# A second expert chosen with the first, and empty rows written as whole rows: layout and request order in a fused attention and mixture-of-experts kernel

## The chip, the cores and the metric

The kernel runs on one core of one Trainium2 chip. The metric is the device time of one execution in microseconds, as the median of several runs; lower is better. Three runs of the kernel before gave 1181.35, 1182.36 and 1184.68 us, so the median is 1182.36 us.

## The reference

The computation has three parts in a row, all in float32.

```python
# attention: x [8,8,512,64], state [8,8,32,64]; scale = 1/8
xread = softmax(scale * x @ state.T) @ state          # 512 rows per batch and head
sread = softmax(scale * state @ x.T) @ x              # 32 rows per batch and head
x = concat([xread, sread], axis=2) -> [8*544, 512]    # heads side by side: 4352 tokens
# first layer: 512 -> 1536 -> 512
x = ((x @ w_a) * (x @ w_b)) @ w_out
# second layer: 8 experts, 512 -> 1024 -> 512, one expert per token
logits = x @ w_gate;  e = argmax(logits, axis=1)
gate = softmax(logits)[e];  eom = sigmoid(x @ w_output_gate)[e]
out[token] = gate * eom * (relu(x @ w1[e]) @ w2[e])
```

The rows that go to each expert depend on the data. With the inputs of the reference the counts of the eight experts are 1082, 32, 576, 64, 512, 1024, 512, 550 over all 4352 tokens, and 1024, 0, 512, 0, 512, 1024, 512, 512 over the 4096 tokens of `xread` alone.

## The kernel before

Phase 1 goes over the 8 batches. For each it computes the attention and the first layer for 512 `xread` tokens; the 8 x 32 `sread` tokens are kept and done together at the end (`main_sr`, 256 tokens). As each group of tokens is done, `Phase1.gate` finds its logits, the expert of each token, a count per expert (`cum`) and so each token's row in `ysort`, a buffer in DRAM that holds the tokens sorted by expert with room for 4608 rows (CAP) per expert. A row is written in four pieces of 130 floats (520 bytes: 128 values of the token, its scale, its number). The layout of `ysort` before is four planes, one per piece: piece `a` of row `r` stands at plane `a`, row `r`. The pieces are scattered from GpSimd by indirect DMAs (L799), 128 pieces each; 136 of them in all, the last eight for the `sread` tokens.

Phase 2 multiplies the sorted rows by the experts' weights, 256 rows at a step, and scatters the results to `out`. Each float32 product is made from a high and a low part, so w1, w2 and the tokens are split by ScalarE (high) and VectorE (low) before use. A half step takes 64 rows. The last step of an expert reads past its last token, so the rows behind each expert's end, 128 of them, are first written with zeros and an invalid token number. That is `pads` (L1059): nine DMAs from the sync engine, one per expert and a second one for the first expert, each 4 x 128 pieces of 520 bytes out of the tile `zrow` (one row of 130 floats per partition, broadcast to the four planes).

Before the phase 2 loop there is a prelude, lines 1777 to 1829, written out by hand, in which two steps (-2 and -1) of the largest expert are run while the counts, the order of the experts and the table of steps are worked out by VectorE in `table`, a generator that the prelude advances stage by stage (`stage()`). The expert of these two steps is chosen earlier, in `early` / `choose` (L858), while `main_sr` still runs, from the counts of the 4096 `xread` tokens: `eoh` marks it, `esel` carries its number and its rows to the sync engine. The sync engine then asks for its w1 and w2 and for its rows (`fetch_pre(0)`, `fetch_pre(1)`).

The sync engine's requests stand in one queue, in this order before the change: w1 of the first expert, `fetch_pre(0)`, w2 of the first expert, `fetch_pre(1)`, then, once the order of all experts is known (third stage of `table`), w2 of the second expert into `raw2` (`load_rank`, L1094), the nine pads, and `fetch_pre(2)`, which reads the rows of step 0. Reads of `ysort` are ordered after all earlier writes to it; the scatters and the pads are declared free of order among themselves (`disjoint`).

The prelude ends with: two of the four splits of the second expert's w2, `turn(0)` (VectorE turns the rows that `fetch_pre(2)` brought), `pre1(3)` (first product, its relu by ScalarE and its low part by VectorE), `parts` (split of the turned rows), the last w2 split, and `pre2(-1, 2)`. `pin` (L657) keeps TensorE, ScalarE, VectorE and the sync engine in the order of the source there. `m.run()` (L1274) then opens one block (L1322) in which each engine runs its own loop with semaphores written by hand. The block is entered by all engines together, when their earlier work is done.

In the loop GpSimd fetches rows (`Phase2.fetch`, L926): four DMAs of 512-byte pieces, one per plane, and one for scale and token number (`gt`). It also issues the scatters to `out`, as it does for the prelude's first step in `preout` (L1054), where the second scatter is ordered behind the first.

Of the kernel before, what the change touches and what calls it, by code (L numbers as in the profile page):

```python
# [18 lines left out]
P = 128  # L19
# [8 lines left out]
NE = 8  # L28
# [4 lines left out]
CAP = NT + 256  # L33
RB = DM // 4 + 2
YW = 16 * RB
PADID = 1 << 20
# [15 lines left out]
class Phase1:  # L52
# [7 lines left out]
    def consts(self):  # L60
# [18 lines left out]
        for g in range(4):  # L79
            sl = slice(32 * g, 32 * g + 32)  # L80
            nc.gpsimd.iota(self.ids[sl, 0 : 16 * NB], [[ST, NB], [1, 4], [P, 4]], base=0, channel_multiplier=4)
            nc.gpsimd.iota(self.ids[sl, 16 * NB :], [[ST, NB]], base=S, channel_multiplier=1)
            nc.gpsimd.memset(self.aoff[sl], float(g * NE * CAP))
# [141 lines left out]

    def disjoint(self, i):
        i = getattr(i, "ins", i)
        self.tc.declare_no_dep(i, group="scatter", reason="disjoint rows")
        self.tc.add_to_no_dep_group("scatter", i)

# [441 lines left out]
    def gate(self, b, T):  # L672
# [116 lines left out]
        def spread():  # L789
            n = 4 * T  # L790
            ps = self.aux("ps_sp")
            nc.tensor.matmul(
                out=ps[:, 0 : 2 * n], lhsT=self.turnto, rhs=st["z"].rearrange("p t g -> p (t g)"), start=True, stop=True
            )
            du = sm("gdu", [n], U32)
            nc.vector.tensor_scalar(out=du, in0=ps[:, 0:n], scalar1=self.aoff[:, 0:1], scalar2=None, op0=ALU.add)
            nc.vector.tensor_copy(out=blocks[:, :, RB - 2 : RB - 1], in_=ps[:, n : 2 * n].unsqueeze(2))  # L797
            for t in range(n):
                self.scatter(  # L799
                    out=self.ysort.rearrange("a r w -> (a r) w"),  # L800
                    out_offset=bass.IndirectOffsetOnAxis(ap=du[:, t : t + 1], axis=0),
                    in_=blocks[:, t, :],
                    in_offset=None,
                    bounds_check=4 * NE * CAP - 1,
                    oob_is_err=False,
                )
# [16 lines left out]
class Phase2:  # L823
# [17 lines left out]
    def early(self):  # L841
# [14 lines left out]
        def choose():  # L856
            self.yin = [ph.yf[:, YW - CH :], ph.yTf[:, 0:CH], ph.yf[:, 0:CH]]
            self.gt = [t(f"gt{i}", [2, 2]) for i in range(4)]  # L858
            step = self.step
# [5 lines left out]
            )  # L865
            mx = t("emx", [1])
            V.tensor_reduce(out=mx, in_=key, axis=AX.X, op=ALU.max)
            self.eoh = t("eoh", [NE])
            V.tensor_tensor(out=self.eoh, in0=key, in1=mx.to_broadcast([P, NE]), op=ALU.is_equal)
            V.tensor_tensor(out=key, in0=self.eoh, in1=self.e8, op=ALU.mult)  # L870
            V.tensor_reduce(out=mx, in_=key, axis=AX.X, op=ALU.add)
            self.esel = t("esel", [2 + NPRE], I32)
            V.tensor_copy(out=self.esel[:, 0:1], in_=mx)
            V.scalar_tensor_tensor(
                out=self.esel[:, 1:], in0=mx.to_broadcast([P, NPRE + 1]), scalar=float(CAP), in1=step, op0=ALU.mult, op1=ALU.add
            )
# [29 lines left out]
    def tiles(self, ctx):  # L906
# [8 lines left out]
        self.tab = p.tile([1, NSTEP, len(FIELDS)], I32, name="tab")  # L915
        self.zrow = p.tile([P, RB], F32, name="zrow")
        self.nc.gpsimd.memset(self.zrow[:, 0 : RB - 1], 0.0)
        self.nc.gpsimd.memset(self.zrow[:, RB - 1 : RB].bitcast(I32), PADID)
# [7 lines left out]
    def fetch(self, e, yin, gt, row, n=2):  # L926

        ys = self.ph.ysort
        rows = P * n if n else HB
        v = ys[:, ds(row, rows), 0 : RB - 2].rearrange("a (t i) x -> a i t x", i=32)  # L930
        x = yin[:, 0 : 4 * rows].rearrange("p (t x) -> p t x", x=P)
        r = [e.dma_start(out=x[32 * a : 32 * a + 32], in_=v[a]) for a in range(4)]  # L932
        v = ys[0, ds(row, rows), RB - 2 : RB]
        if n:
# [124 lines left out]
    def pads(self):  # L1059

        nc = self.nc
        why = "table() bounds every field"
        _, rows = nc.values_load_multi_w_load_instructions(
            self.pad[0:1, 0 : NE + 1],
            engines=[nc.sync.engine],
            min_val=0,
            max_val=NE * CAP - P,
            skip_runtime_bounds_check_because=why,
        )
        for row in rows:  # L1070
            i = nc.sync.dma_start(
                out=self.ph.ysort[:, ds(row, P), :].rearrange("a p w -> p a w"),
                in_=self.zrow.unsqueeze(1).to_broadcast([P, 4, RB]),
            )
            self.ph.disjoint(i)

# [16 lines left out]

    def load_rank(self):  # L1094

        r = self.nc.sync.value_load(self.rtab[0:1, 1:2], min_val=0, max_val=NE - 1)
        self.wload(1, r, self.raw2)

    def table(self, cp):
# [35 lines left out]
        self.pad = cp.tile([P, NE + 1], I32, name="pad")  # L1135
        self.rtab = cp.tile([P, NE], I32, name="rtab")
        pad = t([NE + 1])
# [50 lines left out]
        for v in (nr, gr):  # L1188
            V.tensor_scalar(out=v[:, 0:1], in0=v[:, 0:1], scalar1=1.0, scalar2=None, op0=ALU.max)
        m = t([NE, NE])  # L1190
# [578 lines left out]
def moe_kernel(tc, x, state, w_a, w_b, w_out, w_gate, w_og, w1, w2, out):  # L1769
    w_a, w_b, w_out = (w.bitcast(I32) for w in (w_a, w_b, w_out))  # L1770
    with ExitStack() as ctx:
        pool = lambda n, **k: ctx.enter_context(tc.tile_pool(name=n, bufs=1, **k))
        cp, dp, pg = pool("cp"), pool("dp", space=bass.MemoryType.DRAM), pool("pg")
        ysort = dp.tile([4, NE * CAP, RB], F32, name="ysort")
        ph = Phase1(tc, x, state, w_a, w_b, w_out, w_gate, w_og, ysort, cp, pg)
# [15 lines left out]
        stage()  # L1791
        m.fetch_pre(1)
        m.pre1(0, {15: logits})
        m.pre1(1, {6: gather})
# [70 lines left out]
```

## Time and profile before

The profiled execution took 1187.72 us, of which the span from the first to the last instruction is 1186.0 us; the mean granted TensorE clock is 0.974 of full speed.

| engine | busy us | share of span | instructions |
|---|---|---|---|
| PE (TensorE matmul) | 1123.9 | 95% | 7032 |
| DVE (VectorE) | 648.5 | 55% | 1118 |
| ACT (ScalarE) | 430.1 | 36% | 706 |
| POOL (GpSimd) | 283.9 | 24% | 392 |

The page's 40 slices are 29.65 us each. PE is busy nine tenths or more in nearly all of them; the one slice in the second half that shows less (6 tenths) is the one from 771 to 800 us. The prelude stands from 738 to 796 us and the loop from 798 us to the end. Times in the views below are microseconds from the start of the span; "SPq" is the sync engine's queue, and a bracket at the end of a row gives the engine's idle time ahead of it and what ended it.

### The profile page before, as it was taken

The numbers are of one execution on the slowest core, as the hardware profiler recorded it, in microseconds if no ns is written. First come the engines' busy times: TensorE is split into PE (matmuls) and PEld (weight loads), VectorE is DVE, ScalarE is ACT, GpSimd is POOL, SyncE is SP. The second block draws the span as 40 slices with busy tenths as digits, with TensorE's granted clock in tenths as the row PEclk, the third lists the DMA queues.
The fourth block names the chain that finished last, engine by engine and source line by source line (L and its number), as shares of the span: only waits on it lengthen the run. The fifth ranks groups of instructions, "written<-read, shape, count | busy, mean of one in ns | idle before, by whom it ended". The sixth has DMA issues, their size and how long they took to land. (4 is left out here: it accounts for less than half of the span.)

```text
span 1186.0 us, 19358 instructions
## 1 busy us (share of the span) xinstructions
PE 1123.9 (95%) x7032; PEld 902.4 (76%) x7032; DVE 648.5 (55%) x1118; ACT 430.1 (36%) x706; POOL 283.9 (24%) x392
## 2 busy tenths in 40 slices
PE   3898999999999999999999999969999999999994
PEld 1665777777677777776777799859899998889983
DVE  5889646565464465654754366742442444455463
ACT  4765424333333343333432245321421324142341
POOL 2000005006023050060230524311331232232121
PEclk8898999999999999999999999989999999999997
DMA  6563320302203103020000116369271253536420
GB/s 196 192 226 107 72 38 30 79 3 72 38 15 78 19 30 79 1 72 1 12 26 1 35 33 182 96 128 239 67 204 41 62 166 74 147 89 164 103 97 21
DMA packets 102497, 98.92 MB, mean 83 GB/s; under 512 B 60144, under 2 KB 76048, under 8 KB 102352
## 3 DMA queue, kind: packets, MB, share of 16 engines
q1 hardware_dynamic: 90920, 71.56, 23.2%
q0 software_dynamic: 11168, 25.52, 7.6%
q8 instruction: 72, 1.18, 0.4%
q14 instruction: 73, 0.60, 0.2%
q10 hardware_dynamic: 264, 0.07, 0.0%
HBM read 76.75 MB, written 21.15 MB: 83 GB/s over the span
## 5 line engine op out<-in xcount | busy, mean ns | idle before, releaser
L1009 PE MATMUL ps_h<-yT,w 128*128 128x256 f32 x1536 | 197.5, 285 | 11.0 <-issue 10.0
L1009 PEld LDWEIGHTS ps_h<-yT,w 128*128 128x128 f32 x1536 | 193.9, 193 | 16.8 <-issue 10.8
L1030 PE MATMUL ps_o<-w,hT 128*128 (+1 forms) x768 | 188.1, 394 | 2.3 <-DVE hT L970 2.2
L224 POOL DMA_INDIRECT ysort<-y,gdu x136 | 152.2, 1119 | 149.4 <-DVE y L797 105.8
L528 PE MATMUL ps_y<-gh,wo_h 128*128 128x512 f32 (+1 forms) x432 | 167.1, 392 | 2.1 <-ACT wo_h L218 1.9
L528 PE MATMUL ps_y<-gh,wo_l 128*128 128x512 f32 (+1 forms) x432 | 165.5, 383 | 0.1
L1030 PEld LDWEIGHTS ps_o<-w,hT 128*128 128x128 f32 x768 | 141.5, 190 | 29.8 <-issue 2.4
L528 PE MATMUL ps_y<-gl,wo_h 128*128 128x512 f32 (+1 forms) x432 | 163.3, 379 | 0.0
L516 PE MATMUL ps_ab<-Ah,Mh 128*128 128x512 f32 x384 | 129.6, 418 | 6.8 <-ACT Mh L258 6.8
L501 DVE TENSOR_TENSOR a<-a,ps_ab 128x512 f32<-128x512 f32 x96 | 65.6, 684 | 127.8 <-PE ps_ab L516 126.9
L516 PE MATMUL ps_ab<-Al,Mh 128*128 128x512 f32 x384 | 121.8, 398 | 0.0
L516 PE MATMUL ps_ab<-Ah,Ml 128*128 128x512 f32 x384 | 119.5, 392 | 0.0
L516 PEld LDWEIGHTS ps_ab<-Ah,Mh 128*128 128x128 f32 x384 | 66.7, 191 | 63.1 <-issue 40.2
L990 POOL DMA_INDIRECT out<-yT,gt x37 | 44.6, 1205 | 281.6 <-DVE yT L980 226.7
L964 ACT ACTIVATE hT<-ps_h 128x512 fp32r<-128x512 f32 x64 | 38.0, 593 | 201.5 <-PE ps_h L1009 194.1
L258 ACT ACTIVATE gh<-a 128x512 fp32r<-128x512 f32 (+1 forms) x108 | 65.4, 606 | 106.5 <-DVE a L501 106.5
L528 PEld LDWEIGHTS ps_y<-gh,wo_h 128*128 128x128 f32 x432 | 81.6, 189 | 26.5 <-issue 6.3
L259 DVE TENSOR_TENSOR gl<-a,gh 128x512 fp32r<-128x512 f32 (+1 forms) x108 | 71.1, 658 | 44.6 <-ACT gh L258 44.5
L970 DVE SCALAR_TENSOR_TENSOR hT<-ps_h,hT 128x512 fp32r<-128x512 f32 x64 | 44.0, 687 | 93.7 <-ACT hT L964 93.7
L500 ACT ACTIVATE a<-ps_ab 128x512 f32<-128x512 f32 x96 | 57.5, 599 | 101.4 <-PE ps_ab L516 101.2
L528 PEld LDWEIGHTS ps_y<-gl,wo_h 128*128 128x128 f32 x432 | 81.5, 189 | 16.3
L259 DVE TENSOR_TENSOR Ml<-ps_m,Mh 128x512 fp32r<-128x512 f32 x96 | 61.8, 684 | 56.5 <-ACT Mh L258 56.5
(255 smaller groups left out, 1410.7 us busy)
## 6 DMA issues: line engine op xcount, KB each, us to landing
raw<-in_moe_w SPq DMA_DIRECT2D x32, 512.0 KB, 10.1
raw<-in_moe_w SPq DMA_DIRECT2D x8, 2048.0 KB, 9.6
x<-in_x SPq DMA_DIRECT2D x7, 1024.0 KB, 5.5
xin<-in_x SPq DMA_DIRECT2D x96, 64.0 KB, 2.6
y<-in_moe_w_a SPq DMA_DIRECT2D x8, 512.0 KB, 5.8
yT<-in_moe_w_b SPq DMA_DIRECT2D x8, 512.0 KB
y<-ysort POOLq DMA_DIRECT2D x28, 128.0 KB, 8.6
y<-in_moe_w_out SPq DMA_DIRECT2D x6, 512.0 KB, 5.5
```

The source lines that it names most:

```text
L224: self.disjoint(self.nc.gpsimd.indirect_dma_start(**kw))
L258: self.nc.scalar.activation(out=hi, in_=src, func=AF.Copy)
L259: self.nc.vector.tensor_tensor(out=lo, in0=src, in1=hi.bitcast(F32), op=ALU.subtract)
L500: nc.scalar.activation(out=a[:, 0:n], in_=pa[:, 0:n], func=AF.Copy)
L501: nc.vector.tensor_tensor(out=a[:, 0:n], in0=a[:, 0:n], in1=pb[:, 0:n], op=ALU.mult)
L516: nc.tensor.matmul(out=ps, lhsT=m[:, ab, q, c0 : c0 + P], rhs=r[:, q, :], start=i == 0, stop=i == 5)
L528: nc.tensor.matmul(out=y, lhsT=l[:, f, P * c : P * c + P], rhs=r, start=f == 0 and i == 0, stop=f == NFC - 1 and i == 2,)
L964: return e.activation(out=self.hT[:, j % 2, :, 0, :], in_=self.ps_h[j % 2].rearrange("p (f n) -> p f n", f=2), func=AF.Relu)
L970: return e.scalar_tensor_tensor(out=l, in0=self.ps_h[j % 2].rearrange("p (f n) -> p f n", f=2), scalar=0.0, in1=h.bitcast(F32), op0=ALU.ma ...
L990: return e.indirect_dma_start(out=self.out, out_offset=bass.IndirectOffsetOnAxis(ap=to[0:rows].bitcast(U32), axis=0), in_=self.ob[t][0:row ...
L1009: m = e.matmul(out=self.ps_h[j % 2][:, G * (f % 2) : G * (f % 2) + G], lhsT=self.w1[:, wh, x : x + P], rhs=self.yT[:, c, yh, :], start=k == 0,
L1030: m = e.matmul(out=self.ps_o[2 * (k % 2) + t], lhsT=self.hT[:, j % 2, f, hh, P * t : P * t + P], rhs=self.w2c(slot, wh, 2 * j + f), start= ...
```

## The change

The choice of the first expert also takes the second. `choose` subtracts 2^17 from the key of the first, takes the largest of the rest (`eoh2`) and puts its number into a new last column of `esel`. The sync engine reads that number behind `fetch_pre(1)` and asks for the second expert's w2 there (`second`, which replaces `load_rank`). So that the order of the experts in the table agrees with it, the key of the second is raised by 2^16 in `table`, and the second expert has at least one step.

`ysort` is laid out by rows: the four pieces of a row stand behind one another, 2080 bytes a row. The index of a scattered piece is now 4 x row + piece. `zrow` is a whole row of 520 floats per partition, and each of the nine pad DMAs writes 128 runs of 2080 bytes. The pads are asked in the second stage of `table`, right after the counts are there, and not in the third.

The two scatters to `out` in `preout` are declared free of order between themselves. In the prelude the last split of the second expert's w2 moves from behind `parts` to ahead of `turn(0)`.

```diff
-            nc.vector.tensor_scalar(out=du, in0=ps[:, 0:n], scalar1=self.aoff[:, 0:1], scalar2=None, op0=ALU.add)
+            nc.vector.tensor_scalar(
+                out=du, in0=ps[:, 0:n], scalar1=4.0, scalar2=self.aoff[:, 0:1], op0=ALU.mult, op1=ALU.add
+            )
...
-                    out=self.ysort.rearrange("a r w -> (a r) w"),
+                    out=self.ysort.rearrange("r (a w) -> (r a) w", a=4),
...
+            V.scalar_tensor_tensor(
+                out=self.eoh2, in0=self.eoh, scalar=float(-(1 << 17)), in1=key, op0=ALU.mult, op1=ALU.add
+            )
+            V.tensor_reduce(out=mx2, in_=self.eoh2, axis=AX.X, op=ALU.max)
+            V.tensor_tensor(out=self.eoh2, in0=self.eoh2, in1=mx2.to_broadcast(sh), op=ALU.is_equal)
...
+            V.tensor_tensor(out=key, in0=self.eoh2, in1=self.e8, op=ALU.mult)
+            V.tensor_reduce(out=mx2, in_=key, axis=AX.X, op=ALU.add)
+            self.esel = t("esel", [3 + NPRE], I32)
+            V.tensor_copy(out=self.esel[:, 2 + NPRE :], in_=mx2)
...
-        self.zrow = p.tile([P, RB], F32, name="zrow")
-        self.nc.gpsimd.memset(self.zrow[:, 0 : RB - 1], 0.0)
+        self.zrow = p.tile([P, ROWW], F32, name="zrow")
+        self.nc.gpsimd.memset(self.zrow, 0.0)
...
-        v = ys[:, ds(row, rows), 0 : RB - 2].rearrange("a (t i) x -> a i t x", i=32)
+        v = ys[ds(row, rows), :].rearrange("(t i) (a x) -> a i t x", i=32, a=4)[:, :, :, 0 : RB - 2]
...
-            self.store(self.nc.gpsimd, k, t)
+            self.ph.disjoint(self.store(self.nc.gpsimd, k, t), "out")
...
-    def load_rank(self):
-        r = self.nc.sync.value_load(self.rtab[0:1, 1:2], min_val=0, max_val=NE - 1)
+    def second(self):
+        r = self.nc.sync.value_load(self.esel[0:1, 2 + NPRE :], min_val=0, max_val=NE - 1)
         self.wload(1, r, self.raw2)
...
-            i = nc.sync.dma_start(
-                out=self.ph.ysort[:, ds(row, P), :].rearrange("a p w -> p a w"),
-                in_=self.zrow.unsqueeze(1).to_broadcast([P, 4, RB]),
-            )
-            self.ph.disjoint(i)
+            self.ph.disjoint(nc.sync.dma_start(out=self.ph.ysort[ds(row, P), :], in_=self.zrow))
...
         V.tensor_copy(out=self.pad, in_=pad)
+        self.pads()
...
-        V.scalar_tensor_tensor(out=key, in0=self.eoh, scalar=float(1 << 17), in1=key, op0=ALU.mult, op1=ALU.add)
+        for x, w in ((self.eoh, 1 << 17), (self.eoh2, 1 << 16)):
+            V.scalar_tensor_tensor(out=key, in0=x, scalar=float(w), in1=key, op0=ALU.mult, op1=ALU.add)
...
         er = pick(e8)
-        V.tensor_copy(out=self.rtab, in_=er)
-        self.load_rank()
-        self.pads()
...
         m.fetch_pre(1)
+        m.second()
...
         m.wsplit(1, m.raw2, 2)
+        m.wsplit(1, m.raw2, 3)
         turn(0)
         m.pre1(3)
         m.parts()
-        m.wsplit(1, m.raw2, 3)
         m.pre2(-1, 2)
```

## Rows read from the trace of the kernel before

**Rows 1.** Waits of TensorE from 797 us to the end: total us, times, longest.
```profile
PE ps_h L1009 <- issue: 10.0, 1, 10.0
PE ps_o L1030 <- DVE hT L970: 2.2, 1, 2.2
PE ps_h L1480 <- DVE w L1642: 2.1, 1, 2.1
PE ps_o L1480 <- DVE hT L1670: 2.0, 1, 2.0
```

**Rows 2.** Chain that ended last, 700 to 850 us: start us, us, what.
```profile
794.51 1.24 DVE w L904
...
797.87 4.49 PE ps_h L1009 x24
802.37 2.75 PE ps_o L1030 x12
805.11 2.87 PE ps_h L1009 x24
```

**Rows 3.** Timeline at the end of the prelude: start us, us, engine, line, operation.
```profile
781.12 2.36 DVE L904 TENSOR_TENSOR w<-raw,w 128x1024 fp32r<-128x1024 f32 x2 [0.26 <-ACT w L903]
...
784.96 2.91 PE L1030 MATMUL ps_o<-w,hT 128*128 128x512 f32 x12
785.07 0.98 POOL L990 DMA_INDIRECT out<-yT,gt  x1 [9.35 <-issue]
785.16 0.60 ACT L964 ACTIVATE hT<-ps_h 128x512 fp32r<-128x512 f32 x1 [3.12 <-PE ps_h L1009]
785.55 2.06 SPq L932 DMA_DIRECT2D y<-ysort  x4
...
791.11 1.25 DVE L946 STREAM_TRANSPOSE yts<-y 128x1024 f32<-128x1024 f32 x1 [7.63 <-DMA y<-ysort]
792.28 0.65 DVE L970 SCALAR_TENSOR_TENSOR hT<-ps_h,hT 128x512 fp32r<-128x512 f32 x1
...
793.05 1.29 DVE L961 TENSOR_TENSOR yT<-yts,yT 128x512 fp32r<-128x512 f32 x2
```

**Rows 4.** Waits of the sync engine's queue, 720 to 860 us.
```profile
SPq L932 <- DMA ysort<-zrow: 7.3, 1, 7.3
```

**Rows 5.** Timeline of the sync engine's queue, 690 to 800 us.
```profile
735.15 1.09 SPq L935 DMA_DIRECT2D gt<-ysort  x1
761.68 0.40 SPq L894 DMA_DIRECT2D raw<-in_moe_w  x1
763.32 13.76 SPq L1071 DMA_DIRECT2D ysort<-zrow  x9
```

**Rows 6.** Timeline of GpSimd in the prelude's first microseconds.
```profile
734.11 0.21 POOL L917 MEMSET zrow<- 128x129 f32 x1 [7.49 <-DVE wl L259]
```

**Rows 7.** Timeline of the prelude's middle: the counts, and the last scatter.
```profile
754.05 0.17 DVE L1143 CAST pad<-srT 128x9 int32<-128x9 f32 x1
...
764.22 0.98 POOL L224 DMA_INDIRECT ysort<-y,gdu  x1 [0.30 <-issue]
```

**Rows 8.** Stretches around the pads; last three columns: TensorE clock, DMA share, GB/s.
```profile
767.00:771.00 4.00, 4.00 (x25) 3.51 (x24) 3.55 (x24) 0.60 (x1) 0.00 (x0) 1.00 1.01 326
...
775.00:779.00 4.00, 3.95 (x28) 3.51 (x27) 3.54 (x17) 0.00 (x0) 0.72 (x1) 1.00 1.27 184
```

**Rows 9.** Stretches around TensorE's waits, same columns as Rows 8.
```profile
790.00:792.00 2.00, 0.00 (x0) 0.00 (x0) 0.89 (x1) 0.00 (x0) 0.00 (x0) 0.69 0.03 1
...
1019.30:1022.00 2.70, 2.65 (x7) 2.09 (x8) 2.70 (x4) 0.00 (x0) 0.00 (x0) 0.53 0.00 0
...
1157.50:1160.00 2.50, 2.46 (x11) 2.06 (x12) 2.50 (x3) 2.50 (x5) 0.14 (x1) 1.00 0.27 105
```

**Rows 10.** Timeline of VectorE: one of four transposes that waited for a fetch.
```profile
1016.25 1.25 DVE L946 STREAM_TRANSPOSE yts<-y 128x1024 f32<-128x1024 f32 x1 [5.29 <-DMA gt<-ysort]
```

**Rows 11.** Chain that ended last, 985 to 1026 us.
```profile
1019.35 4.59 PE ps_o L1030 x12
```

More of the change, by code (lines that the diff above doesn't have):

```diff
@@ L34 @@
 RB = DM // 4 + 2
+ROWW = 4 * RB
 YW = 16 * RB
@@ L82, in consts @@
             nc.gpsimd.iota(self.ids[sl, 16 * NB :], [[ST, NB]], base=S, channel_multiplier=1)
-            nc.gpsimd.memset(self.aoff[sl], float(g * NE * CAP))
+            nc.gpsimd.memset(self.aoff[sl], float(g))
             nc.gpsimd.memset(self.own[sl, g : g + 1], 1.0)
@@ L224, in scatter, with disjoint @@
         self.disjoint(self.nc.gpsimd.indirect_dma_start(**kw))
-    def disjoint(self, i):
+    def disjoint(self, i, group="scatter"):
         i = getattr(i, "ins", i)
-        self.tc.declare_no_dep(i, group="scatter", reason="disjoint rows")
-        self.tc.add_to_no_dep_group("scatter", i)
+        self.tc.declare_no_dep(i, group=group, reason="disjoint rows")
+        self.tc.add_to_no_dep_group(group, i)
     def load_x(self, b):
@@ L857, in choose @@
             self.yin = [ph.yf[:, YW - CH :], ph.yTf[:, 0:CH], ph.yf[:, 0:CH]]
-            self.gt = [t(f"gt{i}", [2, 2]) for i in range(4)]
+            gt = t("gt", [4, 2, 2])
+            self.gt = [gt[:, i] for i in range(4)]
             step = self.step
@@ L865, in choose @@
             )
-            mx = t("emx", [1])
+            mx, mx2 = (lambda m: (m[:, 0:1], m[:, 1:2]))(t("emx", [2]))
             V.tensor_reduce(out=mx, in_=key, axis=AX.X, op=ALU.max)
-            self.eoh = t("eoh", [NE])
-            V.tensor_tensor(out=self.eoh, in0=key, in1=mx.to_broadcast([P, NE]), op=ALU.is_equal)
+            self.eoh, self.eoh2 = t("eoh", [NE]), t("eoh2", [NE])
+            sh = [P, NE]
+            V.tensor_tensor(out=self.eoh, in0=key, in1=mx.to_broadcast(sh), op=ALU.is_equal)
+            V.scalar_tensor_tensor(
[3 more added lines that the diff above has]
+            V.tensor_tensor(out=self.eoh2, in0=self.eoh2, in1=mx2.to_broadcast(sh), op=ALU.is_equal)
             V.tensor_tensor(out=key, in0=self.eoh, in1=self.e8, op=ALU.mult)
             V.tensor_reduce(out=mx, in_=key, axis=AX.X, op=ALU.add)
-            self.esel = t("esel", [2 + NPRE], I32)
+            V.tensor_tensor(out=key, in0=self.eoh2, in1=self.e8, op=ALU.mult)
+            V.tensor_reduce(out=mx2, in_=key, axis=AX.X, op=ALU.add)
+            self.esel = t("esel", [3 + NPRE], I32)
+            V.tensor_copy(out=self.esel[:, 2 + NPRE :], in_=mx2)
             V.tensor_copy(out=self.esel[:, 0:1], in_=mx)
             V.scalar_tensor_tensor(
-                out=self.esel[:, 1:], in0=mx.to_broadcast([P, NPRE + 1]), scalar=float(CAP), in1=step, op0=ALU.mult, op1=ALU.add
+                out=self.esel[:, 1 : 2 + NPRE], in0=mx.to_broadcast([P, NPRE + 1]), scalar=float(CAP), in1=step, op0=ALU.mult, op1=ALU.add
             )
@@ L929, in fetch @@
         rows = P * n if n else HB
-        v = ys[:, ds(row, rows), 0 : RB - 2].rearrange("a (t i) x -> a i t x", i=32)
+        v = ys[ds(row, rows), :].rearrange("(t i) (a x) -> a i t x", i=32, a=4)[:, :, :, 0 : RB - 2]
         x = yin[:, 0 : 4 * rows].rearrange("p (t x) -> p t x", x=P)
         r = [e.dma_start(out=x[32 * a : 32 * a + 32], in_=v[a]) for a in range(4)]
-        v = ys[0, ds(row, rows), RB - 2 : RB]
+        v = ys[ds(row, rows), RB - 2 : RB]
         if n:
@@ L1056, in preout @@
             self.gate(self.nc.vector, k, t)
-            self.store(self.nc.gpsimd, k, t)
[L1059 to L1068, printed above, removed]
-        )
-        for row in rows:
-            i = nc.sync.dma_start(
-                out=self.ph.ysort[:, ds(row, P), :].rearrange("a p w -> p a w"),
-                in_=self.zrow.unsqueeze(1).to_broadcast([P, 4, RB]),
-            )
-            self.ph.disjoint(i)
+            self.ph.disjoint(self.store(self.nc.gpsimd, k, t), "out")
     def load(self, e, k, *names):
@@ L1092, in load, with pads @@
         ]
-    def load_rank(self):
-        r = self.nc.sync.value_load(self.rtab[0:1, 1:2], min_val=0, max_val=NE - 1)
+    def second(self):
+        r = self.nc.sync.value_load(self.esel[0:1, 2 + NPRE :], min_val=0, max_val=NE - 1)
         self.wload(1, r, self.raw2)
+    def pads(self):
+        nc = self.nc
+        _, rows = nc.values_load_multi_w_load_instructions(
+            self.pad[0:1, 0 : NE + 1],
+            engines=[nc.sync.engine],
+            min_val=0,
+            max_val=NE * CAP - P,
+            skip_runtime_bounds_check_because="table() bounds every field",
+        )
+        for row in rows:
+            self.ph.disjoint(nc.sync.dma_start(out=self.ph.ysort[ds(row, P), :], in_=self.zrow))
     def table(self, cp):
@@ L1135, in table @@
         self.pad = cp.tile([P, NE + 1], I32, name="pad")
-        self.rtab = cp.tile([P, NE], I32, name="rtab")
         pad = t([NE + 1])
@@ L1187, in table @@
         gr = pick(ng)
-        for v in (nr, gr):
-            V.tensor_scalar(out=v[:, 0:1], in0=v[:, 0:1], scalar1=1.0, scalar2=None, op0=ALU.max)
+        for v, n in ((nr, 2), (gr, 1)):
+            V.tensor_scalar(out=v[:, 0:n], in0=v[:, 0:n], scalar1=1.0, scalar2=None, op0=ALU.max)
         m = t([NE, NE])
@@ L1773, in moe_kernel @@
         cp, dp, pg = pool("cp"), pool("dp", space=bass.MemoryType.DRAM), pool("pg")
-        ysort = dp.tile([4, NE * CAP, RB], F32, name="ysort")
+        ysort = dp.tile([NE * CAP, ROWW], F32, name="ysort")
         ph = Phase1(tc, x, state, w_a, w_b, w_out, w_gate, w_og, ysort, cp, pg)
```

## The prediction, made before the changed kernel was run

> **What bounds the kernel now.** The engine shares of the page come first: PE is busy 95% of the span, so a gain can only come from one of the few places where it stands still. The waits of TensorE are therefore read next. From the end of the prelude to the end of the program there are four worth naming: one of 10.0 us in front of L1009 and three of 2.0 to 2.2 us [rows 1]. The large one is put down to "issue", which names no engine, so the chain of waits is read over that stretch. It runs over VectorE: a split of w2 (L904) takes 1.24 us from 794.51 to 795.75, and the loop's first matmul stands at 797.87 [rows 2]. Of the 2.12 us between them the engines enter their loops and read the table; I call this the entry.
>
> Why VectorE is late is in the timeline [rows 3]. TensorE finishes the prelude at 784.96 + 2.91 = 787.87. VectorE ended two w2 splits at 781.12 + 2.36 = 783.48 and then stands still for 7.63 us until the rows of step 0 land at 791.11; behind that transpose stand the low part of hT, the split of the turned rows (until 794.34) and the last w2 split. The rows land late because their request went out only at 785.55, and it did so because the sync queue waited 7.3 us for the pads [rows 4]. The pads were asked at 763.32, behind w2 of the second expert at 761.68, and the nine of them took the queue 13.76 us to hand out [rows 5]. So the chain is: pads, fetch, transpose, entry; TensorE is idle for 797.87 - 787.87 = 10.0 us at its end.
>
> **Part by part.** *The pads move.* In the changed kernel they need only the counts, which VectorE has converted at 754.05 + 0.17 = 754.22 [rows 7]. From the w2 request to the first pad the queue took 763.32 - 761.68 = 1.64 us [rows 5], in which the nine row numbers were read; I put the same behind 754.22 and have the first pad at 755.9, 7.4 us earlier. Their time: before, from 763.32 to the fetch at 785.55, 22.2 us [rows 3, 5], with the 2 MB of w2 ahead of them in the same queue. Bounds: as long as that although w2 is gone, 22.2 us; or 9 x 128 x 2080 bytes = 2.40 MB at the best rate of that stretch, 326 GB/s, 7.3 us [rows 8]. In between, pads and the eight scatters (another 0.53 MB) at the rate of the stretch that is nearly all pads, 184 GB/s, take 15.9 us, and at 326 GB/s 9.0 us [rows 8]. I take 12 us, since 2080-byte runs should lie nearer to the faster stretch, which is mostly the 2 KB rows of w2; they are landed at 768 (763 to 778). The other condition of the fetch is the last scatter, whose instruction ends at 764.22 + 0.98 = 765.20 [rows 7]; it lands with the pads. So `fetch_pre(2)` goes out at about 768. From its request to the transpose it took 791.11 - 785.55 = 5.56 us [rows 3]: its rows are there at 773.6, in the worst bound at 783.7.
>
> Here a page speaks against the change. Row first: the second scatter to `out`, ordered behind the landing of the first, waited 9.35 us, until 785.07, about when the pads had landed [rows 3]. The Trainium skill, DMA: Bandwidth & Descriptors, section "Queues, rings and completion order", says that the count which reports a transfer as done comes, on each DMA engine, only after every earlier write of that engine, those of other queues included. By that the scatters, which now run among the pads, all report with the pads' end; this case's row agrees. Without the rule the last scatter could report about 3 us after 765.2; by it, at the end of all 2.93 MB, which at the slow rate is 771.8, and the transpose's rows would come at 777.4. The sum stays at 7.75 us by either, but the rule takes 4 us of the cover away and so bears on the first rival.
>
> *What is late next.* VectorE's order is then: two splits until 783.48, the moved third one (1.24 us [rows 2], its ScalarE half in ScalarE's idle 3.12 us) until 784.7, the transpose 1.25 until 785.95. The relu that the low part of hT needs ends at 785.16 + 0.60 = 785.76. From the start of that low part to the end of the turned rows' split VectorE took 794.34 - 792.28 = 2.06 us [rows 3]; 785.95 + 2.06 = 788.0. TensorE ends at 787.87, the same. So the fetch has 784.7 - 773.6 = 11 us to spare (1 in the worst bound), TensorE itself is the bound to the end of the prelude, and with the entry of 2.12 us the loop starts at 790.1: **7.75 us earlier**.
>
> *The clock.* During the idle 10 us the granted clock fell to 0.69 in the stretch from 790 to 792 and was at the lower level (1.2 GHz) when the loop began [rows 9]: the first 24 matmuls took 4.49 us where 2.87 is usual, a loss of 1.62 us [rows 2]. After the change TensorE is idle for some 2.2 us. The rows show both answers to a wait of that length: behind the 2.2 us at 1017 the clock was 0.53 and 12 matmuls took 4.59 us, where such a group takes 2.75, and behind the 2.1 us at 1155 it stayed at 1.00 [rows 1, 2, 9, 11]. So the loss of 1.62 us goes or stays; I count half, **0.8 us**, with 0 and 1.6 as ends.
>
> *The early w2.* It goes out behind `fetch_pre(1)`, whose last request ends at 735.15 + 1.09 = 736.24 [rows 5]. Its tile lies in memory that phase 1's weights held; `zrow`, in the same pool, was written at 734.11 once VectorE had ended its last use there [rows 6], so no wait holds it and the pads behind it. Its 2 MB take 11.4 us at the slow 184 GB/s [rows 8] and land near 748, well ahead of its first two splits' place in the prelude, of which the pair at 781.12 is the second and third [rows 3]. Behind it the queue holds nothing until 754. Cost and gain by itself: 0, its worth is that it is no longer ahead of the pads. That the second expert is the right one can be read from the counts: 1024 against at most 512 after 4096 tokens, 1024 against at most 576 after all; the order of the steps stays.
>
> *Small edits.* Six more VectorE instructions in `choose`, about 0.2 us each by the small cast's 0.17 [rows 7], delay the request for w1 by 1.2 us; its first split stands twelve slots of `main_sr` later (L610, L611). Matmuls need VectorE's splits of the phase 1 weights there, made one round ahead. I count 0, at most 1.2. In `table` one such instruction comes and one cast goes: 0. `zrow` is four times as large, so its memset takes some 0.8 us instead of 0.21 [rows 6], with GpSimd free until the scatters: 0. The two scatters to `out` no longer wait for each other: GpSimd is free 9 us earlier, and the next that it does is in the loop: 0. The scattered pieces have the same size and number as before: 0.
>
> *Fetches in the loop.* They read the same 512-byte pieces, 2080 bytes apart instead of 520. The trace has no such read. Bounds: the one fetch on which TensorE waited (1016.25, TensorE idle 2.2 us) may land earlier, which takes away up to those 2.2 us and the clock's 4.59 - 2.75 = 1.84 behind them, or later by as much, which costs 2.2 [rows 1, 2, 10, 11]. I take 0, nearest to equal sizes and counts. The other three transposes that wait for a fetch cost TensorE nothing now: none of its waits stands behind them [rows 1].
>
> **Sum.** 7.75 + 0.8 = 8.6 us. The profiled execution's 1187.72 becomes 1179.1; its span 1186.0 becomes 1177.4. That execution stands 5.4 us over the median of the runs, and I take the gain as the same in both, so the median 1182.36 becomes **1173.8**.
>
> **Rivals.** *The fetch is still last.* Pads and scatters share the engines, and both report late. Every microsecond that `fetch_pre(2)` goes out after 784.7 - 5.56 = 779.1 is taken from the gain. Out at 783, the gain is 8.6 - 3.9 = 4.7 and the time 1177.7; from 784.2 on it is within 3.5 us of before. For it: pads alone moved only 184 GB/s at a share of 1.27 [rows 8]. Against it: they start 7.4 us earlier without the 2 MB ahead of them.
>
> *The loop's fetches land sooner.* With row-wise storage a step's rows are one piece of DRAM. If that saves 2.2 us at 1016.25, the gain is 8.6 + 2.2 + 1.84 = 12.6 and the time 1169.8. For it: nothing but the layout; against: the pieces are the same.
>
> *The loop's fetches land later, and the kernel is slower.* Place: the four transposes that wait for a fetch [rows 10]. If each of the contested fetches takes x longer and all four pass it on, the cost is 4x, which meets 8.6 at x = 2.2 us; if only the one at 1016.25 does, at 8.6 us. With x = 3.3 at all four the time is 1182.36 - 8.6 + 13.2 = 1187. For it: each row is now touched by four separate DMAs; against: three of the four pass on nothing of their waiting now [rows 1], so they have room.
>
> **How the numbers follow.** The forecast (gain 7 to 10, 1172.4 to 1175.4): 0.62. Fetch still last: 0.23, of it 0.13 with a gain of 3.5 to 7 and 0.10 within 3.5. Loop sooner: 0.08. Loop later: 0.07, slower. About 0.3% (3.5 us) is what a measurement of this kernel tells from no change. That makes faster 0.83, same 0.10, slower 0.07. The range goes from the sooner loop's 1169.8, a little below, to 1179.0, which leaves out the no-gain and slower cases and a small part of the first rival: 1169.5 to 1179.0.
>
> **What would show it.** Right: the pads' first request near 756 and `fetch_pre(2)` well ahead of 779 in the sync queue; the transpose of step 0 directly behind the third split with no wait for a DMA; TensorE's wait in front of L1009 down from 10.0 to about 2.2 us; the loop's length unchanged. Wrong: the sync queue still waiting for `zrow` or a scatter at 780, an entry longer than 2.1 us, or TensorE waits in the loop beyond the present three.

## The result, and the profile after

The changed kernel took 1170.55 us (median of five runs, 1167.5 to 1175.01) against 1182.36 us before (five runs, 1181.12 to 1185.36). The ratio is 0.989, with a 95% interval of 0.9868 to 0.9912: faster, by 10 to 16 us. The prediction was 1173.8 us, a gain of 8.6. The median lies in the range given. But the gain is larger than the terms of the sum give at their upper ends, 7.75 + 1.62 = 9.4 us, so something that the prediction counted as nothing was worth several microseconds. Beside `w2_late` and `hT_even` below, in both runs of each, the kernel before itself took 1215 and 1218 us and not 1182 to 1186, so those kernels are compared only with one another.

In these fences columns and signs are those of the rows of before. First the profile page, whose span and line for the first product of a step (L1009 before, L1022 now; there 197.5 us, 285 ns and 10.0 us of "issue") answer to the table:

```profile
span 1165.8 us, 19364 instructions
...
PE 1111.1 (95%) x7032; PEld 890.7 (76%) x7032; DVE 648.2 (56%) x1124; ACT 430.4 (37%) x706; POOL 283.6 (24%) x392
...
L1022 PE MATMUL ps_h<-yT,w 128*128 128x256 f32 x1536 | 191.7, 281 | 3.0 <-issue 2.0
```

The waits of TensorE from 780 to 1190 us, which answer to [rows 1]:

```profile
PE ps_h L1486 <- DVE w L1648: 2.1, 1, 2.1
PE ps_h L1022 <- issue: 2.0, 1, 2.0
PE ps_o L1043 <- DVE hT L983: 1.8, 1, 1.8
PE ps_o L1486 <- DVE hT L1676: 1.6, 1, 1.6
```

The wait of 10.0 us ahead of the loop is 2.0 us, and the other three are within 0.4 us of before. Why is in the timeline at the end of the prelude, which answers to [rows 3]. Here, L917 is the split of w2, L959 the transpose of the fetched rows, L983 the low part of hT, L974 the split of the turned rows and L1043 the prelude's last product:

```profile
778.03 3.50 DVE L917 TENSOR_TENSOR w<-raw,w 128x1024 fp32r<-128x1024 f32 x3 [0.26 <-ACT w L916]
...
781.45 1.24 DVE L959 STREAM_TRANSPOSE yts<-y 128x1024 f32<-128x1024 f32 x1
...
781.85 2.93 PE L1043 MATMUL ps_o<-w,hT 128*128 128x512 f32 x12
...
782.68 0.69 DVE L983 SCALAR_TENSOR_TENSOR hT<-ps_h,hT 128x512 fp32r<-128x512 f32 x1
...
783.38 1.29 DVE L974 TENSOR_TENSOR yT<-yts,yT 128x512 fp32r<-128x512 f32 x2
...
786.82 4.62 PE L1022 MATMUL ps_h<-yT,w 128*128 128x256 f32 x24 [2.04 <-issue]
```

The transpose has no bracket: VectorE goes from the third split straight to it, where before it stood still for 7.63 us. The sync engine's queue and the counts, which answer to [rows 5, 7]:

```profile
734.12 0.51 SPq L907 DMA_DIRECT2D raw<-in_moe_w  x1
752.36 6.37 SPq L1105 DMA_DIRECT2D ysort<-zrow  x9
763.82 1.96 SPq L945 DMA_DIRECT2D y<-ysort  x4
```

```profile
750.98 0.17 DVE L1150 CAST pad<-srT 128x9 int32<-128x9 f32 x1
...
761.16 0.98 POOL L225 DMA_INDIRECT ysort<-y,gdu  x1 [0.30 <-issue]
```

The counts are converted at 750.98 here and at 754.05 in [rows 7], so this profile is 3.07 us ahead already: early in phase 1 it lost less to clock drops (granted clock 1.00 from 59 to 119 us, 0.91 in the profile before), which vary from run to run (0.97 in the repeated run of the changed kernel). Places are compared after adding 3.07.

### The profile page after: what moved, and what is told of

Read it like the earlier page. It is cut to its first block, busy times and chain, and to the rows that moved or that the text cites. A ratio compares the mean times of both kernels' runs of the same rounds, so it can differ in the third digit from the quotient of the medians.

```text
span 1165.8 us, 19364 instructions
## 1 busy us (share of the span) xinstructions
PE 1111.1 (95%) x7032; PEld 890.7 (76%) x7032; DVE 648.2 (56%) x1124; ACT 430.4 (37%) x706; POOL 283.6 (24%) x392
## 4 chain that ended last, share of the span: by engine, by line
PE 85%; DVE 6%; DMA 3%; ACT 3%; issue 2%; SPq 0%; DVEq 0%; POOL 0%; POOLq 0%; ACTq 0%
PE ps_y L529 22%; PE ps_ab L517 22%; PE ps_h L1022 14%; PE ps_o L1043 14%; PE ps_m L486 4%; PE ps_sab L637 3%; PE ps_h L1486 1%; DMA y<-in_moe_w_a 1%; PE ps_o L1486 1%; DMA gt<-ysort 1%; PE ps_l L691 1%; DVE wab L206 1%; ACT cr L194 1%; PE ps_sr L424 1%; DMA y<-in_moe_w_out 1%
## 5 line engine op out<-in xcount | busy, mean ns | idle before, releaser
L1022 PEld LDWEIGHTS ps_h<-yT,w 128*128 128x128 f32 x1536 | 188.6, 190 | 9.1 <-issue 2.9
L1022 PE MATMUL ps_h<-yT,w 128*128 128x256 f32 x1536 | 191.7, 281 | 3.0 <-issue 2.0
L1043 PE MATMUL ps_o<-w,hT 128*128 (+1 forms) x768 | 187.3, 393 | 2.0 <-DVE hT L983 1.8
L1043 PEld LDWEIGHTS ps_o<-w,hT 128*128 128x128 f32 x768 | 140.0, 188 | 29.6 <-issue 2.0
L983 DVE SCALAR_TENSOR_TENSOR hT<-ps_h,hT 128x512 fp32r<-128x512 f32 x64 | 44.0, 688 | 88.7 <-ACT hT L977 88.6
## 6 DMA issues: line engine op xcount, KB each, us to landing
raw<-in_moe_w SPq DMA_DIRECT2D x32, 512.0 KB, 10.9
```

What stands on the lines that cost most here:

```text
L983: return e.scalar_tensor_tensor(out=l, in0=self.ps_h[j % 2].rearrange("p (f n) -> p f n", f=2), scalar=0.0, in1=h.bitcast(F32), op0=ALU.ma ...
L1022: m = e.matmul(out=self.ps_h[j % 2][:, G * (f % 2) : G * (f % 2) + G], lhsT=self.w1[:, wh, x : x + P], rhs=self.yT[:, c, yh, :], start=k == 0,
L1043: m = e.matmul(out=self.ps_o[2 * (k % 2) + t], lhsT=self.hT[:, j % 2, f, hh, P * t : P * t + P], rhs=self.w2c(slot, wh, 2 * j + f), start= ...
```

## The experiments

All were measured beside the kernel before; ratios are to it, with 95% intervals. Two theories stood against each other for what the prelude does not explain: the loop's fetches land sooner from the row-wise layout, or the loop's matmuls run faster for some other reason. The first four runs separate the parts of the change.

**The changed kernel and the one before, each once more.**

> The changed kernel, not altered. Open is why the loop of phase 2 was 9 us shorter in its profile (first matmul of the loop to the end of the span 379.0 us, 388.1 before), beside the 8.0 us that the wait ahead of the loop lost. In that profile the 24 matmuls of a first product (L1022) followed each other at 113 to 118 ns, before at 120 ns throughout; 60 groups x 23 x 2 to 7 ns are 3 to 9 us. Theory A, the cadence belongs to the kernel (where its tiles stand in memory): 113 to 118 ns again, loop near 379 us. Theory B, the cadence is a matter of the run: any of 113, 117 or 120 ns, and the loop 379 to 388 us with it. Theory C, the row-wise reads: cadence does not matter, the loop is short because fetches land sooner, TensorE's waits in the loop are under 1 us each. All: the wait ahead of the loop 2.0 us; time 1167 to 1175.

> The kernel before, not altered: the second profile of it. Theory A: first products at 120 ns throughout, loop near 388 us. Theory B: 113 to 118 ns may be seen here too, and the loop is then 380 to 385 us. Theory C: loop 388 us whatever the cadence. All: the wait ahead of the loop 10.0 us; time 1181 to 1186.

Measured: 1169.94 us, 0.9873 (0.9849 to 0.9897), and 1185.82 us, 0.9998 (0.9979 to 1.0018). The gain repeats, at 12 to 18 us; the wait ahead of the loop was 2.1 and 10.9 us. The clock shows what a single profile is worth: the loop's first 24 matmuls took 5.39 us here in the kernel before (4.49 in [rows 2]) and 3.00 us in the changed one (4.62 above), after waits of about the same length (10.9 and 10.0 us, 2.1 and 2.0). These are rows of TensorE's timeline in the repeated changed kernel:

```profile
786.58 3.00 PE L1022 MATMUL ps_h<-yT,w 128*128 128x256 f32 x24 [2.12 <-issue]
789.42 2.91 PE L1043 MATMUL ps_o<-w,hT 128*128 128x512 f32 x12
792.16 2.91 PE L1022 MATMUL ps_h<-yT,w 128*128 128x256 f32 x24
```

**The order alone.** The changed kernel with the four planes and the 520-byte pads put back:

```diff
-        self.zrow = p.tile([P, ROWW], F32, name="zrow")
+        self.zrow = p.tile([P, RB], F32, name="zrow")
...
-        ysort = dp.tile([NE * CAP, ROWW], F32, name="ysort")
+        ysort = dp.tile([4, NE * CAP, RB], F32, name="ysort")
```

> Only the order is changed, not the layout: second expert and its w2 early, pads right after the counts, last split moved, the two scatters to out free of each other; rows stay in four planes and each pad DMA writes 4 x 128 runs of 520 bytes. The matmul operands stand at the same addresses as in the changed kernel. My prediction's sum says that the layout is worth nothing: the wait ahead of the loop 2.0 to 2.2 us as in the changed kernel, pads landed a few us later but hidden. Theory A: cadence 113 to 118 ns and time 1167 to 1175 like the changed kernel. Theory B: time between 1167 and 1178, cadence any. Theory C: loop 388 us, so time near 1174 to 1176 and over the changed kernel's in every pair.

Measured: 1172.05 us, 0.9902 (0.9871 to 0.9933). Its sync queue, the queue's wait for the pads, and two stretches of its pads (columns as in [rows 8]):

```profile
736.04 0.41 SPq L905 DMA_DIRECT2D raw<-in_moe_w  x1
754.26 9.30 SPq L1104 DMA_DIRECT2D ysort<-zrow  x9
775.20 2.00 SPq L943 DMA_DIRECT2D y<-ysort  x4
```

```profile
SPq L943 <- DMA ysort<-zrow: 10.5, 1, 10.5
```

```profile
756.00:760.00 4.00, 4.00 (x31) 3.74 (x30) 3.55 (x17) 0.35 (x1) 2.96 (x4) 1.00 1.17 182
760.00:764.00 4.00, 3.80 (x21) 3.01 (x20) 3.72 (x6) 2.70 (x4) 3.39 (x3) 1.00 1.32 155
```

From first pad to fetch: 775.20 - 754.26 = 20.9 us, against 763.82 - 752.36 = 11.5 us with runs of 2080 bytes. Still the transpose waits for nothing: by the 5.56 us of [rows 3] its rows are there at 780.8, and VectorE comes to it at 783.32. TensorE's wait is 2.1 us. The operands of the two products lie where they lie in the changed kernel, and the gain is the same within the intervals, with the old planes: the row-wise fetches are not where the rest of the gain comes from.

**The layout alone.** The requests and the split stand at their old places; rows and pads are 2080 bytes.

```diff
-        self.pads()
...
         er = pick(e8)
+        V.tensor_copy(out=self.rtab, in_=er)
+        self.second()
+        self.pads()
...
-        m.second()
...
-        m.wsplit(1, m.raw2, 3)
...
         m.parts()
+        m.wsplit(1, m.raw2, 3)
```

> Only the layout is changed: rows of 2080 bytes, pads in runs of 2080 bytes, index 4 x row + piece, while w2 of the second expert and the pads are asked in the third stage, as before, and the last split and the order of the scatters to out are as before. The second expert is still worked out with the first, but its early number is not used. By the prediction the fetch ahead of the loop still goes out late: the pads need 7 to 16 us behind the 2 MB of w2, so it goes out at 778 to 785 and the wait ahead of the loop is 4 to 10 us; time 1176 to 1182 without a change of cadence. Theory A: operands stand at a third address, cadence open. Theory C: loop near 379 us and time 1168 to 1174.

Measured: 1178.6 us, 0.9939 (0.9919 to 0.996). Its sync queue and the end of its prelude:

```profile
763.04 0.40 SPq L907 DMA_DIRECT2D raw<-in_moe_w  x1
764.68 9.71 SPq L1105 DMA_DIRECT2D ysort<-zrow  x9
779.83 1.96 SPq L945 DMA_DIRECT2D y<-ysort  x4
```

```profile
784.95 1.24 DVE L959 STREAM_TRANSPOSE yts<-y 128x1024 f32<-128x1024 f32 x1
...
789.34 1.23 DVE L917 TENSOR_TENSOR w<-raw,w 128x1024 fp32r<-128x1024 f32 x1
...
792.66 4.62 PE L1022 MATMUL ps_h<-yT,w 128*128 128x256 f32 x24 [3.19 <-issue]
```

Here too the transpose has no bracket: even from the old place, 2080-byte pads let the rows arrive in time. What is left of the wait, 3.2 us and not 2.0, is the last w2 split behind L974, at its old place. So the two parts of the change overlap: either alone removes the wait for the rows. The whole time is 6.6 us longer than with the order alone, but that can't be put down to the layout: this kernel's operands lie at a third place, and its loop has the slowest pace of all, as the next part shows.

**Placement.** What else differs is where tiles lie in SBUF. The change merges four small tiles into one, which the prediction passed over:

```diff
-            self.gt = [t(f"gt{i}", [2, 2]) for i in range(4)]
+            gt = t("gt", [4, 2, 2])
+            self.gt = [gt[:, i] for i in range(4)]
```

The tile `rtab`, which is gone, and `eoh2`, which is added, cancel each other, so by the merging `yT` and `hT` (the moving operands of the two products) move from bytes 59360 and 67552 of each partition to 59296 and 67488; w1 and w2 stay (these are the places that the programs were laid out with). The layout alone has both `rtab` and `eoh2`, so there they lie at 59328 and 67520. Two kernels separate this from the rest. `gt_one` is the kernel before with the edit above and nothing else, so `yT` lies at 59296. `shift64` is the changed kernel with an unused tile ahead of `gt`, so `yT` lies at 59360 as before:

```diff
+            t("room", [16])
```

> The kernel before, with one edit that belongs to the change and does no work: the four small gt tiles are one tile, so every tile behind them moves by 64 bytes, and the operands of phase 2 stand where they stand in the changed kernel (yT at byte 59296 of a partition instead of 59360, hT at 67488 instead of 67552; w1 and w2 do not move). Theory A (the cadence comes with the place): first products at 113 to 118 ns instead of 120, second products at 229 to 231 instead of 227, the loop (first to last matmul) 365 to 370 us instead of 372 to 375, the wait ahead of it still 10 to 11 us; time 3 to 7 us below the kernel before. Theory B' (the cadence comes with what the change does, the place is chance): 120 ns, time as before.

> The changed kernel with an unused tile of 64 bytes ahead of gt, so that the operands of phase 2 stand where they stood before the change (yT at 59360, hT at 67552). Theory A: first products at 120 ns, second ones at 227, loop 372 to 375 us, the wait ahead of the loop 2.0 us; time 1173 to 1178, which is the gain of 8 us that the prelude alone gives. Theory B': 113 to 118 ns and 1168 to 1172.

Measured: `gt_one` 1181.59 us, 0.9976 (0.9959 to 0.9992); `shift64` 1174.58 us, 0.9922 (0.9909 to 0.9936). Look at the starts of successive groups in TensorE's timeline, in a stretch of the loop at full clock: the distance from one first product to the next is what a half step costs. First `shift64`, then the changed kernel, `gt_one` and the layout alone:

```profile
864.31 3.04 PE L1023 MATMUL ps_h<-yT,w 128*128 128x256 f32 x24
867.19 2.91 PE L1044 MATMUL ps_o<-w,hT 128*128 x12
869.93 3.04 PE L1023 MATMUL ps_h<-yT,w 128*128 128x256 f32 x24
```

```profile
863.77 2.91 PE L1022 MATMUL ps_h<-yT,w 128*128 128x256 f32 x24
866.51 2.91 PE L1043 MATMUL ps_o<-w,hT 128*128 x12
869.26 2.91 PE L1022 MATMUL ps_h<-yT,w 128*128 128x256 f32 x24
```

```profile
867.13 2.99 PE L1010 MATMUL ps_h<-yT,w 128*128 128x256 f32 x24
869.96 2.93 PE L1031 MATMUL ps_o<-w,hT 128*128 x12
872.73 2.99 PE L1010 MATMUL ps_h<-yT,w 128*128 128x256 f32 x24
```

```profile
865.56 3.01 PE L1022 MATMUL ps_h<-yT,w 128*128 128x256 f32 x24
868.41 2.96 PE L1043 MATMUL ps_o<-w,hT 128*128 x12
871.21 3.00 PE L1022 MATMUL ps_h<-yT,w 128*128 128x256 f32 x24
```

The half step is 869.93 - 864.31 = 5.62 us with `yT` at its old place, 5.49 us in the changed kernel, 5.60 us in `gt_one` and 5.65 us in the layout alone. In the kernel before the same stretch reads

```profile
864.57 3.04 PE L1009 MATMUL ps_h<-yT,w 128*128 128x256 f32 x24
867.44 2.91 PE L1030 MATMUL ps_o<-w,hT 128*128 x12
870.19 3.04 PE L1009 MATMUL ps_h<-yT,w 128*128 128x256 f32 x24
```

again 5.62 us. Between the old place and the new one the difference lies almost alone in the first product: at full granted clock its 24 matmuls start 120 ns apart at the old place, in every profile with it, and 113 to 118 ns apart at the new one. The second product's groups take 2.75 us at both, up to 2.77 in the slower stretches of the new one. At the new place there are two paces, 113 ns (5.49 us a half step) and 118 ns (5.59 us), and a run changes between them: the repeated changed kernel runs at 5.50 us around 795 us and at 870.61 - 865.02 = 5.59 us later.

So 64 bytes of placement explain the rest, as far as the intervals tell. There are 1536 / 24 = 64 such groups in the program; at 0.03 to 0.13 us each that is 2 to 8 us. Added up over the 48 to 50 half steps of each profile's loop that nothing interrupts, the time saved against 5.62 us is 4.5 us in the changed kernel, 2.0 in its repeated run, 2.5 in `gt_one`, 0.0 in `shift64` and -1.0 in the layout alone. `gt_one` alone shows 1 to 5 us, barely clear of none, and `shift64`, the change without it, 8 to 11 us. Their sum by the medians' ratios, 2.8 + 9.2 = 12.0 us, is near the change's 13.0 and 15.0, each with an interval of some 5 us.

**Other placements.** If 64 bytes matter, another place may be better. `hT_back` puts `hT` at its old place again, with `yT` at the new one; `yT_even` puts `yT` at 59392, a multiple of 128; `hT_even` puts `hT` at 67584, a multiple of 128 too, with `yT` at the new place.

```diff
+        p.tile([P, 16], F32, name="room")
```

(between `yT` and `hT`, for `hT_back`; 24 floats there for `hT_even`, and 24 on each side of `yT` for `yT_even`.)

> The changed kernel with an unused tile of 64 bytes between yT and hT: yT stays at 59296, hT goes back to 67552, where second products took 227 ns. Theory A with each operand for itself: first products 113 to 118 ns and second ones 227 ns, loop 1 to 2.5 us shorter than in the changed kernel (60 groups of 12 at 2 to 4 ns), time 1167 to 1170. If only the place of all together counts, no difference or a longer loop.

> The changed kernel with unused tiles of 96 bytes ahead of and behind yT: yT at 59392, a multiple of 128, hT at 67680, which is 96 above one as in the kernel before. Theory A: a fourth cadence of the first products, between 107 ns (256 columns at 2.4 GHz) and 121; second ones 227. By itself the theory does not say which; it says that all groups have it, from the prelude to the end. Time 1165 to 1178.

> The changed kernel with an unused tile of 96 bytes between yT and hT: yT stays at 59296, hT goes to 67584, a multiple of 128. If the place of hT sets the pace of the second products, a third value beside 227 ns (hT at 67552) and 229 to 231 (67488); a pair of first and second product takes 5.49 or 5.59 us in the changed kernel and 5.62 before, and this one should lie between 5.45 and 5.65 in every step. Theory that only yT counts: first products at 113 or 118 ns, second at 229 to 231, as in the changed kernel, and its time, 1168 to 1172.

> A second run of the changed kernel with 96 bytes of unused space between yT and hT: yT stays at byte 59296, hT goes to 67584, a multiple of 64. In the first run the kernel before took 1215 us and not 1184. Theory 1: the address of yT alone sets the time of the first product's matmuls and that of hT does nothing: ratio as the changed kernel, 0.987 to 0.990, loop 365 to 370 us. Theory 2: hT's address counts for itself: the groups of the second product are other than 2.75 us by 0.05 us or more in most of the loop, and the time moves by 2 us or more from the changed kernel's 1170.

Measured: `hT_back` 1169.81 us, 0.9877 (0.986 to 0.9894), a half step of 5.55 us; `yT_even` 1173.37 us, 0.9908 (0.989 to 0.9925), a half step of 5.59 us. `hT_back` and `shift64`, measured side by side, are the closest pair: both have `hT` at 67552, and `yT` and what lies ahead of it, back to `gt`, differ by 64 bytes; the times are 1169.81 and 1174.58 us, and the intervals do not meet. `hT_even` gave 0.9952 (0.993 to 0.9973) and 0.9917 (0.9888 to 0.9945), with a half step of 867.44 - 861.91 = 5.53 us in the second run:

```profile
861.91 2.90 PE L1023 MATMUL ps_h<-yT,w 128*128 128x256 f32 x24
864.64 2.96 PE L1044 MATMUL ps_o<-w,hT 128*128 x12
867.44 2.90 PE L1023 MATMUL ps_h<-yT,w 128*128 128x256 f32 x24
```

Its first product is the shortest of all (2.73 us from start to start), but its second takes 2.80 and not 2.75: `hT`'s place counts too. It may also bear on the pace of the first product: with `yT` at 59296 the loop's first products start 118 ns apart in all groups of `hT_back` and 113 ns apart in all groups but one of the two `hT_even` profiles. The rounder address of `yT_even` is not better, and neither it nor `hT_back` beats the placement of the changed kernel by more than the intervals; `hT_even`'s times can't be set against them.

**The second expert's w2 asked behind the pads.** The order alone, with the request for w2 put back into the third stage of `table`, behind the pads, to see whether the early w2 is needed for itself:

```diff
         er = pick(e8)
+        self.second()
         yield
...
         m.fetch_pre(1)
-        m.second()
```

> The order kernel (four planes, operands placed as in the changed kernel), with one thing put back: w2 of the second expert is asked in the third stage of the table, behind the pads and ahead of the fetch, although its number is known early. The pads stay early. My theory says that the early w2 is what makes the early pads worth something: the 2 MB now stand between the pads and the fetch in the sync queue, the pads' nine requests take the queue about 9 to 10 us from 754 (9.30 in the order kernel), w2 goes out near 764 and lands, behind the pads in the DMA queues, near 775 to 782. ScalarE's first split of it stands at 770 to 774 and everything behind it on ScalarE and VectorE waits, so TensorE loses 2 to 8 us ahead of that place or at the entry; the time is 2 to 8 us over the order kernel's. Rival: the early pads alone are the gain, w2 is in time wherever it is asked: no TensorE wait but the 2.1 us at the entry, time equal to the order kernel's (1172).

> A second run of the kernel with only the order changed (four planes, 520-byte pads, w2 of the second expert chosen with the first) in which w2 of the second expert is asked behind the pads and not ahead of them. In the first run the kernel before took 1215 us and not 1184, so it told little. Theory 1: only the pads' place ahead of w2 counts. Then the pads still go out near 754, the fetch of step 0 near 775, TensorE's wait ahead of the loop is 2 to 4 us, and the ratio is 0.990 to 0.992 as for the order alone. Theory 2: the early request for w2 is needed by itself. Behind the pads it lands too late for its first split at 778, VectorE and ScalarE wait for it, the wait ahead of the loop is 5 us or more and the ratio 0.994 to 1.000.

Measured: 0.9999 (0.9975 to 1.0023) and 0.9995 (0.9968 to 1.0022), 7 and 9 us longer than `hT_even` beside it, which also has the 2080-byte rows. The sync queue, ScalarE and TensorE in the second run:

```profile
802.81 0.79 SPq L905 DMA_DIRECT2D raw<-in_moe_w  x1
```

```profile
822.46 1.06 ACT L914 ACTIVATE w<-raw 128x1024 fp32r<-128x1024 f32 x1 [7.01 <-DMA raw<-in_moe_w]
```

```profile
834.42 5.48 PE L1020 MATMUL ps_h<-yT,w 128*128 128x256 f32 x24 [5.38 <-issue]
```

ScalarE could split it only from 822.46, 7.0 us after it was ready to, and the loop starts behind a wait of 5.4 us (2.1 in `hT_even`, both runs; 3.9 in the first run of this kernel). So with pads of 520 bytes the early w2 is needed for itself: behind them it becomes the late one. That is only a part of the 7 and 9 us: from the counts to the loop's start the two profiles take 41.8 and 43.9 us, those of `hT_even` 40.5 and 40.3. What the rest is was not shown: the two kernels differ in the layout and in `hT`'s place as well. What the late w2 costs where the kernel before takes 1184 us was not measured.

## Why the prediction was right in the prelude and wrong in size

*The chain pads, fetch, transpose, entry: right.* With 3.07 us added for the head start, each step stands where it was put. The first pad was predicted at 755.9 and went out at 755.4; `fetch_pre(2)` 768 and 766.9; the transpose 784.7 and 784.5; the loop 790.1 and 789.9, which makes 8.0 us for the term of 7.75. The entry is 786.82 - (783.38 + 1.29) = 2.15 us (2.12 used). From first pad to fetch, taken as 12 us between 7.3 and 22.2, it was 11.5 us. That is in part luck, since 12 us was meant for the pads, and the queue's wait ahead of the fetch, the second of these two, was for the last scatter:

```profile
SPq L945 <- DMA ysort<-y,gdu: 9.2, 2, 5.7
```

No wait for `zrow` stands ahead of the fetch any more: the pads were done before that scatter. 2080-byte runs moved at 359 GB/s, and the 324 GB/s from 760 to 761 us fell to 108 in the next microsecond, which makes about 9 us for the pads:

```profile
756.00:760.00 4.00, 3.80 (x27) 3.31 (x26) 3.79 (x10) 0.70 (x2) 3.09 (x4) 1.00 1.01 359
```

In the order alone, 520-byte runs among the same scatters moved at 130 to 182 GB/s from 756 to 772 us, and its 20.9 us lie near the upper bound.

*The first rival, the fetch still last: not there.* The fetch went out at 766.9 on the old axis, 12 us ahead of the 779.1 from which it decides. The rule of the Trainium skill that was weighed for it (DMA: Bandwidth & Descriptors, "Queues, rings and completion order") cost nothing: the fetch followed the end of the last scatter's instruction, 762.14, by 1.7 us. With 520-byte pads the median scatter needed 11.0 us to land against 4.4 us here and 2.8 before. That fits the rule, but pads that take the engines' time would do the same, and no run separates the two; even the 11.0 us were hidden.

*The clock: open, as put.* Half of 1.62 us was counted. Behind waits of 2.0 to 2.1 us the loop's first group took 4.6 us in six profiles (the first one after, `shift64`, `hT_back`, `yT_even` and both of `hT_even`) and 3.00 in two (the repeated run, the order alone). The kernel before, behind its 10 us, took 4.49 and 5.39. So the term was worth between nothing and 2.4 us.

*Early w2, small edits in `choose`, `zrow`, the scatters: right at 0*, as far as the chain shows; nothing waits for them. The moved w2 split was read rightly too: at its old place, as in the layout alone, it costs 3.2 - 2.0 = 1.2 us, its own length.

*The loop's fetches sooner or later: neither.* In the profile after, TensorE's waits of about 2 us are the same three, and the order alone has the gain with the old planes. What both rivals were priced by, the wait of 2.2 us behind the fetch of 1016.25 [rows 1, 10], is not in the second profile of the kernel before, whose waits from 780 us on are 10.9, 2.1 and 1.7 us: it came and went with the run.

*The step that failed is "the loop's length unchanged".* It stood on instructions and transfers being the same. The instructions are, but their operands lie 64 bytes lower, and the first product of each half step takes 2.75 to 2.83 us from start to start in place of 2.87. That is the part of the gain beyond the prelude, as near as the intervals tell: `shift64`, which has the whole change but that, gains 9.2 us (7.6 to 10.8), as the sum of 8.6 had it; the change itself 13.0 and 15.0. The edit that did it, the merging of `gt`, appears in no term of the sum. That the median lies in the stated range is luck: the range reaches down to 1169.5 for the sooner loop's sake, and the forecast by itself was 1172.4 to 1175.4. One profile against one profile would have misled: they differ by 20.2 us, of which 8.0 lie at the entry, 9.1 behind the loop's start (1186.0 - 797.87 against 1165.8 - 786.82) and 3.1 ahead of the counts. But 1186.0 - 797.87 = 388.1 us is itself 3.2 us more than the repeated run of the same kernel has there (1185.4 - 800.44): the 2.2 us at 1017 and the 1.84 us lost behind them are in it, less 0.9 us for a first group that was slower in the repeated run. Only kernels that isolate the placement settled its share.

*Open:* why the pace of the first product depends on the byte at which its moving operand lies, and what picks one of the two paces at one address (`hT`'s place may, by one profile of `hT_back` and two of `hT_even`).

## What to carry to other kernels

Follow the wait that ends last back through every queue it passes, and ask for what does not depend on the late result ahead of what does: the forecast of such a chain, step by step with the bounds of the one unknown, came out within about a microsecond, one of its terms for another reason than the one given. Two remedies for one wait don't add up: here order alone or larger runs alone took it away, and the rest of each was slack. When an edit adds, drops or merges tiles, look at which operands of the bound engine move, and keep a variant with the old addresses before a gain or a loss is put down to the edit's purpose.

## What the runs showed of the hardware

- The pace of back-to-back matmuls of 256 columns with a new weight tile each depends on where the moving operand lies in SBUF: 120 ns with `yT` at byte 59360, 113 or 118 ns at 59296, 117 to 118 ns at 59328 and 116 to 118 ns at 59392, at full granted clock and with the weights in the same place.
- Zero rows written to DRAM in runs of 2080 bytes moved at 359 GB/s at a DMA share of 1.01; in runs of 520 bytes at 130 to 182 GB/s at a share of 1.17 to 1.32; scatters of 520-byte pieces were among both.
- A pause of TensorE of 2.0 to 2.1 us ahead of the loop left the first group at 3.00 us in two profiles and made it 4.6 us in six others of nearly the same program.
